# k of batch 2 transposed by DMA instead of by TensorE, with three loads held behind it, and whole loads for batch 0

## The chip, the cores and the metric

The kernel runs on one core of one Trainium2 chip. The metric is the device time of one execution in microseconds (us). Three runs of the kernel before gave 250.74, 250.46 and 250.03, median 250.46. A profile of one execution goes with it.

## The reference

Two attentions in a row, then a feed-forward layer with the gate h·cos(h). Batch 8, 8 heads, sequence 576, head size 64, 32 packed queries; 4608 tokens, model width 512, inner width 2048.

```python
def sm_attn(qq, kk, vv):
    s = scale * np.matmul(qq, kk.transpose(0, 1, 3, 2))
    s = s - np.max(s, axis=-1, keepdims=True)
    a = np.exp(s)
    a = a / (np.sum(a, axis=-1, keepdims=True) + 1e-09)
    return np.matmul(a, vv)
p_packed = sm_attn(p, k, v)
out = sm_attn(q, p_packed, p_packed)        # [8, 8, 576, 64]
x = out.transpose(0, 2, 1, 3).reshape(4608, 512)
h = x @ w_in
g = h * np.cos(h)
result = g @ w_out                          # [4608, 512], float32
```

## The kernel before

The work goes by batch, eight of them, in a pipeline written out by hand: nothing is reordered by a scheduler, so each engine executes its instructions in the order of the source. Matmuls are in bf16.

For a batch b, `load` brings k, q or v from DRAM with a cast to bf16 into the tiles `kbf` (two buffers), `qbf` and `vbf` (one buffer each). These DMAs are issued by POOL (L87). k and q must be transposed so that the head dimension lies on partitions: the tiles `kT` (two buffers) and `qT` (one). There are two ways. `xbar` (L94 to L96) issues one transposing DMA from SP, called a crossbar transfer here. `pe_T` (L98) lets TensorE (PE) do it in groups of 128x96 blocks into PSUM, each group followed by a copy on DVE or ACT. `permute_v` copies v into the tile `vp`.

The first attention is `s1` (scores against the packed queries, exp on ACT), a transposition of its result to `a1T` (`a1_pe` and `a1_one` on PE, `a1_xbar` by a DMA from SP, L159) and `pp` (L186, a1T times vp). The second is `s2` (scores of q, exp), `sums2`, `normalise`. The packed values are multiplied into w_in first (`ppw`), giving the tile `PPW`. Then `h_mm` (L259) makes one of 16 blocks of h, ACT takes the cosine (L263), DVE forms the product gT (L266). The last matmuls, with w_out (L312), come from a generator `out_gen`, and `fill(n)` puts n of them where PE would otherwise wait. Their results are copied to `osb` (four buffers) and stored by DMAs from SP (L319). The PSUM pool psA has three buffers.

A "slot" s is the loop over the 16 blocks of h of batch s, in which `hooks` run work for the next batches at given blocks. Between slots stand `s1`, `s2`, `ppw` and others, with fills.

POOL issues the loads, and also copies (`vp` of some batches, a `joint` tile). A `gate` is a tiny POOL copy that reads one element of a `kT`: since POOL executes in order, the loads behind it are issued only once that transposed tile has landed. `next_loads` in slot 1 (L449) does this for q of batch 3, k of 4 and v of 3; L504 and L530 do it for later ones. SP likewise executes its transposing DMAs and stores in order.

At the start, `warm(n)` runs n matmuls on zeros. k and q of batch 0 are each loaded in two DMAs of four heads and transposed on PE in four groups of six blocks. k of batch 2 is loaded at L408 and v of 2 at L410, both before slot 0; q of 2 and k of 3 are loaded ahead of slot 1. In slot 1, the hooks 5, 6 and 7 transpose k of batch 2 on PE, a group of eight blocks each with a copy on DVE. Hook 4 issues the crossbar transfers of q of 2 and k of 3.

Of the kernel before, what the change touches and what calls it, by code (L numbers as in the profile page):

```python
# [15 lines left out]
def kernel(  # L16
# [11 lines left out]
    B, H, S, D = q.shape  # L28
# [4 lines left out]
    C = 6  # L33
    TP = S // C
# [20 lines left out]
    V, ACT, G = nc.vector, nc.scalar, nc.gpsimd  # L55
# [5 lines left out]
    gate = const.tile([1, 1], BF16, name="gate")  # L61
# [7 lines left out]
    srcs = {"k": k, "q": q, "v": v}  # L69
    bf, vp, xT, a1T, sums1, r1, rs1 = {}, {}, {}, {}, {}, {}, {}  # L70
    a2u, lns, a2n, PPW = {}, {}, {}, {}

    def copy(eng, out, in_):
        if eng is ACT:
            ACT.copy(out=out, in_=in_)  # L75
        else:
            eng.tensor_copy(out=out, in_=in_)  # L77

    def psa(dt=FP32):
        return A.tile([128, 2, 512 if dt == FP32 else 1024], dt, name="psA", tag="A")  # L80

    def load(n, b, parts=1):
        bf[n, b] = bf_pool.tile([TP, H, C * D], BF16, name=n + "bf", tag=n + "bf", bufs=2 if n == "k" else 1)
        src = srcs[n][b].rearrange("h (p c) d -> p h (c d)", c=C)
        for i in range(parts):
            r = slice(i * H // parts, (i + 1) * H // parts)
            G.dma_start(out=bf[n, b][:, r], in_=src[:, r])  # L87

    def permute_v(b, eng=G):
        vp[b] = vp_pool.tile([TP, C, H * D], BF16, name="vp", tag="vp")  # L90
        copy(eng, vp[b].rearrange("p c (h d) -> p c h d", h=H),
             bf["v", b].rearrange("p h (c d) -> p c h d", c=C))

    def xbar(n, b):  # L94
        t = xT[n, b] = att_pool.tile([128, H * 3, TP], BF16, name=n + "T", tag=n + "T", bufs=2 if n == "k" else 1)
        nc.sync.dma_start_transpose(out=t, in_=bf[n, b].rearrange("p h x -> p (h x)"))  # L96

    def pe_T(n, b, engs=(V, V, V), groups=(0, 1, 2), own=False, m=8):  # L98
        if 0 in groups:
            xT[n, b] = att_pool.tile([128, H * 3, TP], BF16, name=n + "T", tag=n + "T", bufs=2 if n == "k" else 1)  # L100
        t = xT[n, b]
        flat = bf[n, b].rearrange("p h x -> p (h x)")
        for i in groups:
            ps = bank(BF16) if own else psa(BF16)[:, 0, :]
            for j in range(m):
                o = m * i + j
                nc.tensor.transpose(ps[:, j * TP:(j + 1) * TP], flat[:, o * 128:(o + 1) * 128],  # L107
                                    ident[0:TP, 0:TP])
            copy(engs[i], t[:, m * i:m * i + m].rearrange("p a x -> p (a x)"),
                 ps[:, 0:m * TP])  # L110

    def bank(dt=FP32):
        return O.tile([128, 512 if dt == FP32 else 1024], dt, name="ot", tag="ot")

    def pack_p(b0, b1, flat=None):
        ng = 2 * (b1 - b0)
        if flat is None:
            flat = psa(BF16).rearrange("p a x -> p (a x)")
        for g in range(ng):
            nc.tensor.transpose(flat[:, g * 128:(g + 1) * 128],  # L120
                                p_bf[:, 2 * b0 + g].rearrange("p t d -> p (t d)"), ident)
        V.tensor_copy(out=P2[:, b0:b1].rearrange("p b h n -> p (b h n)"), in_=flat[:, 0:ng * 128])

    def scores(lhs, rhs):
        ps = []
        for y in range(2):
            t = psa()
            for x in range(4):
                for e in range(2):
                    r = slice(64 * e, 64 * e + 64)  # L130
                    h = 2 * x + y
                    nc.tensor.matmul(t[32 * x:32 * x + 32, e, 0:HS], lhs[r, h, :],  # L132
                                     rhs[r, 3 * h:3 * h + 3, :], start=True, stop=True)
            ps.append(t)
        return ps

    def s1(b, later=False):
        ps = scores(P2[:, b], xT["k", b])
        sm = sums1[b] = small.tile([128, 2], FP32, name="sums1")

        def exps():
            for y in range(2):
                ACT.activation(  # L143
                    out=a1[b % 2][:, y, :, 0:TP].rearrange("p (e m) x -> p e m x", e=2),
                    in_=ps[y][:, :, 0:HS].rearrange("p e (m x) -> p e m x", m=3),
                    func=AF.Exp, scale=scale, accum_out=sm[:, y:y + 1])
        if later:
            return exps
        exps()

    def recips(b):
        r1[b] = small.tile([128, 2], FP32, name="r1")
        rs1[b] = small.tile([128, 2], FP32, name="rs1")
        V.reciprocal(r1[b], sums1[b])
        V.tensor_scalar(out=rs1[b], in0=r1[b], scalar1=scale, scalar2=None, op0=ALU.mult)  # L155
# [3 lines left out]
        nc.sync.dma_start_transpose(out=t.rearrange("p a c x -> p (a c) x"),  # L159
                                    in_=a1[b % 2].rearrange("p a c x -> p (a c x)"))  # L160

    def a1_pe(b, ys=(0, 1), own=False, eng=V):
        if 0 in ys:
            a1T[b] = att_pool.tile([128, 2, C, 128], BF16, name="a1T", tag="a1T")
        t = a1T[b]
        for y in ys:
            ps = bank(BF16) if own else psa(BF16)[:, 0, :]
            for c in range(C):
                nc.tensor.transpose(ps[0:TP, c * 128:(c + 1) * 128], a1[b % 2][:, y, c, 0:TP], ident)
            copy(eng, t[0:TP, y].rearrange("p c x -> p (c x)"), ps[0:TP, 0:C * 128])  # L170

    def a1_one(b):
        t = a1T[b] = att_pool.tile([128, 2, C, 128], BF16, name="a1T", tag="a1T")
# [155 lines left out]
    def fill(n):  # L329
        while n > 0 and filler[1] > 0:  # L330
            next(filler[0])
            filler[1] -= 1
            n -= 1

    def load_w_in(n):
        G.dma_start(out=w_in_bf[:, :, n * 512:(n + 1) * 512],
                    in_=moe_w_in.rearrange("(a p) n -> p a n", p=128)[:, :, n * 512:(n + 1) * 512])
# [5 lines left out]
    def dup_p(a, b, eng):  # L343
        for t in range(2):
            eng.tensor_copy(out=p_bf[:, a:b, t, :], in_=p_raw[:, a:b, :])

    def warm(n):
        wps = bank()
        for _ in range(n):
            nc.tensor.matmul(wps, wz[:, 0:128], wz, start=True, stop=True)  # L350

    nc.sync.dma_start(out=p_raw[:, 0:2, :], in_=p_rows[:, 0:2, :])
    load("k", 0, 2)
    load("v", 0)
    make_identity(nc, ident)
    load("q", 0, 2)
    load("k", 1)
    for n in range(3):
        load_w_in(n)
# [9 lines left out]
    warm(7)  # L369
    dup_p(0, 2, V)  # L370
    pack_p(0, 1)
    warm(6)
    pe_T("k", 0, (V, ACT, ACT, V), (0, 1), m=6)
    warm(2)
    pe_T("k", 0, (V, ACT, ACT, V), (2, 3), m=6)
    ACT.dma_start(out=p_raw[:, 2:4, :], in_=p_rows[:, 2:4, :])
    s1(0)
    load("v", 1)
    load_w_in(3)
    warm(3)  # L380
    a1_pe(0, (0,))
    permute_v(0, V)
    a1_pe(0, (1,), eng=ACT)
    warm(2)
    recips(0)
    pe_T("q", 0, (V, ACT, V, V), (0, 1), m=6)
    pp(0)
    pe_T("q", 0, (V, ACT, V, V), (2, 3), m=6)
    load("q", 1)
    for n in range(4):  # L390
        load_w_out(n)
# [15 lines left out]
    a1_one(1)  # L407
    load("k", 2)  # L408
    permute_v(1)
    load("v", 2)  # L410
    for fc in range(NFC):
        rest = h_mm(0, fc)
        if fc in (11, 12, 13):
# [13 lines left out]
    def slot(s, hooks, keep=0, heavy={}):  # L427
        left = filler[1] - keep
        out_eng[:] = (ACT,) if s > 1 else (V, ACT)
        weight = [1 + heavy.get(fc, 0) for fc in range(NFC)]  # L430
        for fc in range(NFC):
            h_mm(s, fc)()
            quota = (left * sum(weight[:fc + 1])) // sum(weight) - (left + keep - filler[1])
            first = quota
            while hooks and hooks[0][0] == fc:
                if first == quota and fc in heavy:
                    first = quota // 2
                    fill(first)
                hooks.pop(0)[1]()
            fill(quota - first if first != quota else quota)  # L440

    def pw2(b, n=0, eng=None):
        ppw(b, n, eng)
        ppw(b, n + 1, eng)

    def tk(n, b, i):
        return lambda: pe_T(n, b, (V, V, V), (i,))

    def next_loads():  # L449
        G.tensor_copy(out=gate, in_=xT["k", 3][0:1, 0, 0:1])  # L450
        for n, b in (("q", 3), ("k", 4), ("v", 3)):
            load(n, b)
# [2 lines left out]
    fill(4)  # L455
    s2(1)
    ppw(1, 0, V)
    load("q", 2)
    load("k", 3)
    dup_p(4, 2 * B, G)  # L460
    fill(5)
    sums2(1, 0)
    sums2(1, 1)
# [2 lines left out]
    normalise(1)  # L466
    ACT.preload_act_table_set(SIN_SET)
    fill(14)
    slot(1, [(3, lambda: pw2(1, 2, (ACT, V))), (4, lambda: (xbar("q", 2), xbar("k", 3))), (5, tk("k", 2, 0)), (6, tk("k", 2, 1)),
             (7, tk("k", 2, 2)), (9, lambda: pack_p(2, 5)),  # L470
             (11, lambda: pack_p(5, B)), (12, next_loads)], 4, {3: 3})

    ACT.preload_act_table_set(EXP_SET)
# [3 lines left out]
    s1(2)  # L477
    fill(5)
    a1_pe(2, (0,))
    fill(2)  # L480
    a1_pe(2, (1,))
# [96 lines left out]
```

The softmax here doesn't subtract the row's maximum and nothing guards it: scores larger than these inputs give would overflow.

## Time and profile before

| what | value |
|---|---|
| runs, median | 250.46 us (250.03 to 250.74) |
| profiled execution, its own time | 250.74 us |
| its span in the profile | 249.0 us |
| PE / DVE / ACT / POOL busy | 95% / 67% / 67% / 22% of the span |
| DMA queue of POOL's loads | 23184 packets, 18.75 MB |
| DMA queue of SP's transfers and stores | 39568 packets, 17.83 MB |
| matmuls with w_out, L312 (512 with gT) | 133.3 us, 380 ns each |
| matmuls of h, L259 (512) | 83.8 us, 286 ns each |
| crossbar transfers of q / k / a1 | 6 / 5 / 5, landing 5.5 / 5.3 / 4.0 us after issue (medians) |

The busy time of PE overlaps within itself, because matmuls are pipelined and their ends are modelled. A DMA has two times: how long the issuing engine is held by it, and when its data lands. DMA shares are means over 16 engines. "Idle before" a group of instructions, with what ended it, is harmless on an engine on which nothing waits.

### The profile page before, as it was taken

To read this page: it belongs to the slowest core of one execution; us is meant where nothing else is said; L and a number is where in the kernel's file an instruction comes from. 1 tells how busy PE (TensorE), PEld (TensorE's weight loads), DVE (VectorE), ACT (ScalarE), POOL (GpSimd) and SP (SyncE) were. 2 spreads that over 40 slices of the span, in tenths; PEclk is the share of its full clock that TensorE was granted. 3 is DMA by queue.
4 is the path that set the end of the run, shared out by engine and by line. 5 is a ranking of instruction groups with operands and counts; after the bars stand their busy time and mean duration, and the time that the engine had idled before them with its cause. 6 is when DMAs were issued, how large, how long until landed. Compare 5 with 4: busy or idle time off the path is not lost.

```text
span 249.0 us, 5072 instructions
## 1 busy us (share of the span) xinstructions
PE 236.5 (95%) x2036; PEld 131.1 (53%) x2036; DVE 167.9 (67%) x254; ACT 167.9 (67%) x280; POOL 55.9 (22%) x70
## 2 busy tenths in 40 slices
PE   8868799999999999999999999999999999999993
PEld 3445364566544655465546554565456554665452
DVE  2348997789667977587857666678766774876110
ACT  2558899756656788788867867888777684873000
POOL 8343543240400043113322205020500000000000
PEclk9999999999999999999999999999999999999999
DMA  6999999999899989999989995999491113202133
GB/s 99 167 203 205 205 206 225 202 240 164 170 190 201 185 156 217 205 204 160 200 168 195 165 205 68 190 171 190 94 154 40 45 42 77 52 21 63 46 84 84
DMA packets 63207, 37.09 MB, mean 149 GB/s; under 512 B 35824, under 2 KB 58608, under 8 KB 63184
## 3 DMA queue, kind: packets, MB, share of 16 engines
q0 software_dynamic: 23184, 18.75, 49.5%
q1 hardware_dynamic: 39568, 17.83, 34.2%
q8 instruction: 16, 0.26, 0.4%
q10 hardware_dynamic: 432, 0.20, 0.4%
q14 instruction: 7, 0.06, 0.1%
HBM read 37.22 MB, written 9.44 MB: 187 GB/s over the span
## 4 chain that ended last, share of the span: by engine, by line
PE 71%; DMA 15%; DVE 6%; ACT 3%; POOL 2%; issue 1%; DVEq 0%; POOLq 0%
PE ot L312 43%; PE psA L259 19%; DMA w_out_bf<-in_moe_w_out_dram 8%; DMA w_in_bf<-in_moe_w_in_dram 7%; DVE gT L266 4%; PE psA L210 3%; ACT cosT L263 2%; PE psA L186 2%; PE psA L132 2%; PE ot L298 1%; PE psA L236 1%; DVE PPW L77 1%; POOL kbf L87 1%; ACT ppT L75 1%; DVE a2n L246 1%
## 5 line engine op out<-in xcount | busy, mean ns | idle before, releaser
L312 PE MATMUL ot<-w_out_bf,gT 128*128 128x512 bf16 x512 | 133.3, 380 | 0.1
L266 DVE TENSOR_TENSOR gT<-psA,cosT 128x576 bf16<-128x576 f32 x128 | 93.7, 756 | 26.5 <-ACT cosT L263 25.9
L263 ACT ACTIVATE cosT<-psA 128x576 bf16<-128x576 f32 x128 | 82.5, 651 | 28.2 <-PE psA L259 23.5
L259 PE MATMUL psA<-a2n,PPW 128*128 128x288 bf16 x512 | 83.8, 286 | 1.7 <-DVE PPW L77 0.4
L312 PEld LDWEIGHTS <-gT 128*128 128x128 bf16 x512 | 47.6, 98 | 43.3 <-issue 6.7
L259 PEld LDWEIGHTS <-PPW 128*128 128x128 bf16 x512 | 49.2, 97 | 35.2 <-issue 4.4
L77 DVE CAST PPW<-psA 128x1024 bf16<-128x1024 f32 (+1 forms) x23 | 26.9, 1176 | 11.6 <-PE psA L210 11.5
L270 POOL COPY joint<-gT 128x512 bf16<-128x512 bf16 x16 | 9.8, 614 | 88.1 <-DVE gT L266 88.1
L77 DVE COPY osb<-ot 128x512 f32<-128x512 f32 (+1 forms) x24 | 16.3, 679 | 17.5 <-PE ot L312 13.9
L75 ACT COPY osb<-ot 128x512 f32<-128x512 f32 (+1 forms) x13 | 7.3, 565 | 15.3 <-PE ot L312 10.6
L77 POOL COPY vp<-vbf 96x3072 bf16<-96x3072 bf16 x6 | 16.5, 2749 | 4.0 <-DMA vbf<-in_v_dram 4.0
L246 DVE SCALAR_TENSOR_TENSOR a2n<-a2u,r,lns 128x576 bf16<-128x576 bf16 x16 | 12.3, 813 | 7.3 <-ACT lns L244 7.3
L143 ACT ACTIVATE a<-psA 128x576 bf16<-128x576 f32 x16 | 10.3, 646 | 7.3 <-PE psA L132 7.2
L238 ACT ACTIVATE lns<-psA 128x576 f32<-128x576 f32 x16 | 10.1, 650 | 7.1 <-PE psA L236 6.5
L312 PE MATMUL ot<-w_out_bf,joint 128*128 128x512 bf16 x48 | 12.8, 379 | 0.0
L228 ACT ACTIVATE a2u<-psA,rs 128x576 bf16<-128x576 f32 x16 | 11.0, 737 | 1.5 <-PE psA L132 1.4
L210 PE MATMUL psA<-w_in_bf,ppT 64*32 64x512 bf16 x224 | 10.2, 381 | 0.0
L244 ACT ACTIVATE lns<-lns 128x576 f32<-128x576 f32 x16 | 10.0, 676 | 0.0
L350 PE MATMUL ot<-wz 128*128 128x512 bf16 x24 | 8.8, 500 | 1.2 <-DVE wz L361 1.2
L75 ACT CAST ppT<-psA 64x128 bf16<-64x128 f32 x24 | 6.2, 259 | 5.1 <-DVE ppT L77 3.8
L87 POOL DMA_DIRECT2D vbf<-in_v_dram x8 | 6.2, 776 | 6.4 <-DVE rs L155 4.4
L77 DVE COPY kT<-psA 128x768 bf16<-128x768 bf16 (+1 forms) x8 | 4.0, 526 | 5.2 <-PE psA L107 5.2
(73 smaller groups left out, 153.1 us busy)
## 6 DMA issues: line engine op xcount, KB each, us to landing
vbf<-in_v_dram POOLq DMA_DIRECT2D x8, 576.0 KB, 8.4
out_dram<-osb SPq DMA_DIRECT2D x24, 192.0 KB, 2.6
kbf<-in_k_dram POOLq DMA_DIRECT2D x7, 576.0 KB, 13.0
qbf<-in_q_dram POOLq DMA_DIRECT2D x7, 576.0 KB, 10.1
out_dram<-osb SPq DMA_DIRECT2D x22, 128.0 KB, 2.4
w_in_bf<-in_moe_w_in_dram POOLq DMA_DIRECT2D x4, 512.0 KB, 17.0
w_out_bf<-in_moe_w_out_dram POOLq DMA_DIRECT2D x4, 512.0 KB, 20.5
out_dram<-osb SPq DMA_DIRECT2D x26, 64.0 KB, 2.1
```

The source lines that it names most:

```text
L75: ACT.copy(out=out, in_=in_)
L77: eng.tensor_copy(out=out, in_=in_)
L143: ACT.activation(out=a1[b % 2][:, y, :, 0:TP].rearrange("p (e m) x -> p e m x", e=2), in_=ps[y][:, :, 0:HS].rearrange("p e (m x) -> p e m ...
L210: nc.tensor.matmul(ps[y][32 * x:32 * x + 32, :], ppT[b % 2][r, 2 * x + y, :], w_in_bf[r, x, n * 512:(n + 1) * 512], start=True, stop=True)
L228: ACT.activation(out=a2u[b][:, y].rearrange("p (e x) -> p e x", e=2), in_=ps[y][:, :, 0:HS], func=AF.Exp, scale=rs1[b][:, y:y + 1])
L238: ACT.activation(out=lns[b][:, y].rearrange("p (e x) -> p e x", e=2), in_=ps[:, :, 0:HS], func=AF.Ln)
L244: ACT.activation(out=lns[b][:, y], in_=lns[b][:, y], func=AF.Exp, scale=-1.0)
L246: V.scalar_tensor_tensor(out=a2n[b][:, y], in0=a2u[b][:, y], scalar=r1[b][:, y:y + 1], in1=lns[b][:, y], op0=ALU.mult, op1=ALU.mult)
L259: nc.tensor.matmul(ps[:, e, 0:HS], PPW[b][:, y, fc * 128:(fc + 1) * 128], a2n[b][:, y, e * HS:(e + 1) * HS], start=(y == 0), stop=(y == 1))
L263: ACT.activation(out=csv, in_=ps[:, :, 0:HS], func=AF.Sin, bias=PI_HALF)
L266: V.tensor_tensor(out=gT[b][:, fc, :].rearrange("p (e x) -> p e x", e=2), in0=ps[:, :, 0:HS], in1=csv, op=ALU.mult)
L312: nc.tensor.matmul(pss[c], w, w_out_bf[:, fc, :], start=(fc == 0), stop=(fc == NFC - 1))
```

## The change

k and q of batch 0 are loaded by one DMA each, and transposed in three groups of eight blocks instead of four of six. The copy of v of batch 0 to `vp` on DVE moves ahead of the a1 transposes, whose two copies are both on DVE. `pp(0)` precedes all transposes of q of batch 0 instead of standing between two halves of them. There are nine warm matmuls ahead of k's transposes instead of six and two.

`xbar("k", 2)` is issued behind `permute_v(1)`, and the three groups `tk` in slot 1 are gone. The loads of v of 2, q of 2 and k of 3 come after `dup_p(4, 2 * B, G)` and behind a POOL copy that reads kT of batch 2.

```diff
-    def load(n, b, parts=1):
+    def load(n, b):
         bf[n, b] = bf_pool.tile([TP, H, C * D], BF16, name=n + "bf", tag=n + "bf", bufs=2 if n == "k" else 1)
-        src = srcs[n][b].rearrange("h (p c) d -> p h (c d)", c=C)
-        for i in range(parts):
-            r = slice(i * H // parts, (i + 1) * H // parts)
-            G.dma_start(out=bf[n, b][:, r], in_=src[:, r])
+        G.dma_start(out=bf[n, b], in_=srcs[n][b].rearrange("h (p c) d -> p h (c d)", c=C))
...
-    load("k", 0, 2)
+    load("k", 0)
     load("v", 0)
     make_identity(nc, ident)
-    load("q", 0, 2)
+    load("q", 0)
...
-    warm(6)
-    pe_T("k", 0, (V, ACT, ACT, V), (0, 1), m=6)
-    warm(2)
-    pe_T("k", 0, (V, ACT, ACT, V), (2, 3), m=6)
+    warm(9)
+    pe_T("k", 0, (V, ACT, V))
     ACT.dma_start(out=p_raw[:, 2:4, :], in_=p_rows[:, 2:4, :])
     s1(0)
+    permute_v(0, V)
     load("v", 1)
     load_w_in(3)
     warm(3)
-    a1_pe(0, (0,))
-    permute_v(0, V)
-    a1_pe(0, (1,), eng=ACT)
+    a1_pe(0)
     warm(2)
     recips(0)
-    pe_T("q", 0, (V, ACT, V, V), (0, 1), m=6)
     pp(0)
-    pe_T("q", 0, (V, ACT, V, V), (2, 3), m=6)
+    pe_T("q", 0, (V, ACT, V))
...
     load("k", 2)
     permute_v(1)
-    load("v", 2)
+    xbar("k", 2)
...
     s2(1)
     ppw(1, 0, V)
-    load("q", 2)
-    load("k", 3)
     dup_p(4, 2 * B, G)
+    G.tensor_copy(out=gate, in_=xT["k", 2][0:1, 0, 0:1])
+    for n, b in (("v", 2), ("q", 2), ("k", 3)):
+        load(n, b)
...
-    slot(1, [(3, lambda: pw2(1, 2, (ACT, V))), (4, lambda: (xbar("q", 2), xbar("k", 3))), (5, tk("k", 2, 0)), (6, tk("k", 2, 1)),
-             (7, tk("k", 2, 2)), (9, lambda: pack_p(2, 5)),
+    slot(1, [(3, lambda: pw2(1, 2, (ACT, V))), (4, lambda: (xbar("q", 2), xbar("k", 3))), 
+             (9, lambda: pack_p(2, 5)),
              (11, lambda: pack_p(5, B)), (12, next_loads)], 4, {3: 3})
```

More of the change, by code (lines that the diff above doesn't have):

```diff
@@ L96, in xbar, with pe_T @@
         nc.sync.dma_start_transpose(out=t, in_=bf[n, b].rearrange("p h x -> p (h x)"))
-    def pe_T(n, b, engs=(V, V, V), groups=(0, 1, 2), own=False, m=8):
+    def pe_T(n, b, engs=(V, V, V), groups=(0, 1, 2), own=False):
         if 0 in groups:
@@ L104, in pe_T @@
             ps = bank(BF16) if own else psa(BF16)[:, 0, :]
-            for j in range(m):
-                o = m * i + j
+            for j in range(8):
+                o = 8 * i + j
                 nc.tensor.transpose(ps[:, j * TP:(j + 1) * TP], flat[:, o * 128:(o + 1) * 128],
                                     ident[0:TP, 0:TP])
-            copy(engs[i], t[:, m * i:m * i + m].rearrange("p a x -> p (a x)"),
-                 ps[:, 0:m * TP])
+            copy(engs[i], t[:, 8 * i:8 * i + 8].rearrange("p a x -> p (a x)"),
+                 ps[:, 0:8 * TP])
     def bank(dt=FP32):
@@ L160, in a1_xbar, with a1_pe @@
                                     in_=a1[b % 2].rearrange("p a c x -> p (a c x)"))
-    def a1_pe(b, ys=(0, 1), own=False, eng=V):
+    def a1_pe(b, ys=(0, 1), own=False):
         if 0 in ys:
@@ L169, in a1_pe @@
                 nc.tensor.transpose(ps[0:TP, c * 128:(c + 1) * 128], a1[b % 2][:, y, c, 0:TP], ident)
-            copy(eng, t[0:TP, y].rearrange("p c x -> p (c x)"), ps[0:TP, 0:C * 128])
+            copy(V, t[0:TP, y].rearrange("p c x -> p (c x)"), ps[0:TP, 0:C * 128])
     def a1_one(b):
@@ L444, in pw2 @@
         ppw(b, n + 1, eng)
-    def tk(n, b, i):
-        return lambda: pe_T(n, b, (V, V, V), (i,))
     def next_loads():
```

## Prediction

> **What bounds the kernel now.** I read the page first. TensorE (PE) is busy 95% of the span, but the DMA row is nearly as full: nine tenths or more in most slices up to 187 us. The chain that ended last is PE work with one long DMA stretch at the start.
>
> ```profile
> PE 236.5 (95%) x2036; PEld 131.1 (53%) x2036; DVE 167.9 (67%) x254; ACT 167.9 (67%) x280; POOL 55.9 (22%) x70
> DMA  6999999999899989999989995999491113202133
> PE 71%; DMA 15%; DVE 6%; ACT 3%; POOL 2%; issue 1%; DVEq 0%; POOLq 0%
> ```
>
> So there are two near-limits, and the change moves work from PE to the DMA side. The next view is the timeline of slot 1 on DVE (start, duration, engine, line, operation). Each PE transposition of k2 leaves a copy on DVE between two gT products:
>
> ```profile
> 53.23 0.55 DVE L77 COPY kT<-psA 128x768 bf16<-128x768 bf16 x1
> 54.03 0.76 DVE L266 TENSOR_TENSOR gT<-psA,cosT 128x576 bf16<-128x576 f32 x1 [0.25 <-ACT cosT L263]
> 54.70 0.55 DVE L77 COPY kT<-psA 128x768 bf16<-128x768 bf16 x1
> ```
>
> The last view is the timeline of SP and POOL for the transfers (SPq is SP's queue; the duration is how long SP is held):
>
> ```profile
> 56.55 3.68 SPq L96 DMA_TRANSPOSE qT<-qbf  x1
> 60.28 3.07 SPq L96 DMA_TRANSPOSE kT<-kbf  x1
> 65.25 0.18 POOL L450 COPY gate<-kT 1x1 bf16<-1x1 bf16 x1 [8.30 <-DMA kT<-kbf]
> 65.79 0.77 POOL L87 DMA_DIRECT2D qbf<-in_q_dram  x1 [0.36 <-issue]
> 73.40 5.95 SPq L96 DMA_TRANSPOSE qT<-qbf  x1
> 79.44 2.43 SPq L159 DMA_TRANSPOSE a1T<-a  x1
> 86.34 0.86 PE L186 MATMUL psA<-a1T,vp 96*128 96x64 bf16 x24 [0.58 <-DVE gT L266]
> ```
>
> This is a chain: q2 and k3 transposed, the gate opens when kT of batch 3 has landed, then q3, k4 and v3 are loaded, then q3 and a1 of batch 3 are transposed, and pp(3) on PE (L186, 86.34) reads that a1T. The tile views, restricted to one issue each, give landings: k2 49.57, v2 52.5, q2 56.5, k3 59.4, kT of 3 65.2, q3 73.4 (7.6 after issue), v3 80.4, a1T of 3 84.84 (5.4 after issue). pp(3) therefore has only 86.34 − 84.84 = **1.5 us of slack**.
>
> **What the Trainium skill says.** "DMA: Bandwidth & Descriptors", section "Issuing engines are not separate DMA queues": transfers from all issuers run on the same 16 engines and interleave. The trace agrees: the crossbar transfer of a q or k landed 4.9 us after issue with its loads landed, 5.5 beside one remaining load, 10.3 beside two. The same page, "Terms" and "DMA Transpose (X-bar)": a plain transposing DMA comes from SP or ACT only, so the new one must stand in SP's order. "TensorE: Matmul & The Clock Gate", Part 1: after an idle window of some 3.4 us the array falls to half clock, and needs about as long to return. The trace shows the cold state at the start (128x512 matmuls 0.43 us apart from 1.2 us on, against 15.32/71 = 0.216 late); no long idle later in this kernel shows the fall.
>
> **The change part by part.**
>
> 1. *Start: k and q of batch 0 whole.* k0's second half landed at 2.07 + 5.8 = 7.9; the same bytes in one DMA land near 7.9. All 24 transposes (50 ns each, 1.2) then come after it instead of 12 (0.68), and the last copy is 0.55 instead of 0.46: +0.6 at the exps. q0's halves landed at 13.0 and 14.8; whole, 24 transposes and the last copy end near 16.6 instead of 16.2: +0.4. Moving the vp copy (0.96 on DVE) before the a1T copies, and both of those to DVE, gives at most as much. POOL issues two DMAs fewer (about 0.6 each saved), but its queue is backlogged (w_in landed 14 to 18 us after issue), so nothing lands sooner. PE then waits for DMA anyway: k1 at 18.8 (0.4), w_in at 31.3 (0.65), w_out at 44.5 (0.2). What arrives at slot 1: taken as 0, bounds −0.3 to +0.6.
>
> 2. *No PE transposes in slot 1.* 24 matmuls at about 43 ns (0.34 us a group of eight) = 1.0 us of PE, and 3 x 0.55 = 1.65 us of DVE. The three steps with a group of transposes took 1.48 us each (51.18, 52.66, 54.14, 55.61); steps with two fills take 0.92. Gain 3 x 0.56 = **−1.7 us** at the end of slot 1, by itself on the path.
>
> 3. *kT of 2 by crossbar.* In SP's order it is the first thing after p_raw, ahead of four stores (issued 47.9 before). k2 lands at about 49.6 as before, since what is queued ahead of it is unchanged. No q or k transfer of this trace runs entirely alone; the nearest is kT of 3: SP 3.07, landing 4.9 (bounds 4.0, the median of a1's, and 5.7). I take 4.9: **54.5**. Its reader, s1(2), runs at 64.7: hidden with 10 us to spare. The four stores go out near 53 to 55; four output buffers cover the four chunks of batch 0, so PE does not feel it.
>
> 4. *The gate.* v2, q2, k3 were issued at 32.8, 39.9, 40.65 and queued behind other loads without a hole. Now POOL waits for kT of 2; behind the gate stand those loads, the vp copy of batch 2, a joint copy and the next gate. From 54.5 the first load is issued 0.55 later (65.2 to 65.79 is the model), v2 at 55.0, q2 at 55.8, k3 at 56.6. In the three groups of v, q, k after 88 us, v landed 6.2, 8.1, 6.5 after its issue, q 9.0, 10.7, 10.1, k 12.1, 13.0, 12.2. Stores are mostly out of the way, so I take 6.2 and 9.0: v2 61.2, **q2 64.8**, and k3 2.9 later as before, 67.7. vp of 2 is then ready at 61.2 + 2.75 = 64.0; pp(2) stands at 68.2 (66.5 with the gain): hidden.
>
> 5. *What comes late next.* The q2 transfer holds SP 64.8 to 68.5 (3.68, again one load beside it) and lands at 70.3; s2(2) ran at 70.53, wanted 68.8 with the gain: the gain is already swallowed. The k3 transfer starts at 68.5 and lands at **73.4**, 8.2 later than before; s1(3) ran at 72.31, so PE is now 1.1 behind. The next gate opens at 73.4; q3 is issued at 74.0 and lands at 81.6; its transfer holds SP 5.95 (k4 and v3 still loading, as before) to 87.55; a1 goes at 87.65 and lands 5.4 later at **93.0**. v3 lands near 88.6, so the vp copy of batch 3 on DVE (84.68 before) waits too, and three psA buffers are full behind it, but this ends before 93.0. pp(3) moves from 86.34 to 93.0: **+6.7 us**. PE executes in order and has nothing else to run there, so the wait is idle time.
>
> 6. *Clock.* That idle lasts about 87 to 93. If the array cools, roughly 3.4 us of half clock cost 1.7. Bounds 0 and 1.7; I take 0.8.
>
> Beyond it, kT of 4 lands at 87.7 + 8.3 = 96.0, q4 near 107, while its transfer would start at 99.98 + 6.7 = 106.7: chain and PE are level again, and pp(4) has 110.35 − 107.65 = 2.7 slack. PE has hardly any idle later from which to win the time back. Sum: 6.7 + 0.8 = +7.5; parts 1 and 2 don't add, because absolute landings decide. The profiled execution took 250.74 (249.0 span and 1.7 around it), 0.28 over the median: 258.2, or **258.0** against the median.
>
> **Rivals.** *A, hidden transfers, faster:* only the −1.7 of slot 1 counts, 248.8. For it: k2's transfer itself has 10 us of cover, and DMA idles between. Against: it needs kT of 3 by 70.6 and a1T of 3 by 84.6, and the group of loads alone takes 12 us. *B, shorter chain:* first load 6.0 after issue and the others 2.6 apart, transfers 3.0 on SP as at 124.9, q3 and a1 nearer to the uncontended 3.7 and 3.9: pp(3) slips 2.5 to 4, no cooling; 253 to 254.5. *C, the delay grows:* loads at the slow end (q 10.7, 1.7 later), q4's transfer late by over pp(4)'s 2.7, full cooling: 260.5 to 262. *D, a wash:* the stall only eats the gain, 250.5.
>
> **Chances.** Main case (255.5 to 260.5) 0.66, B 0.14, C 0.10, A 0.06, D 0.04. About 0.3% (0.75 us) can be told from no change. Faster 0.06, same 0.04, slower 0.90. Range 253.5 to 261.0: it takes in bounds of loads, start and clock, most of B and part of C, and leaves out some 0.2.
>
> **What would show it.** Right: kT of 2 landing near 54.5; v2, q2, k3 issued from 55; the kT of 3 landing near 73.4; the gate at L440 ending its wait there; a PE gap ahead of pp(3) (L183 in the changed numbering) ended by a1T or vp, 5 us or more; slot 1 shorter by 1.7. Wrong: pp(3) waiting under 2 us, q2 landing before 61, or a1T of 3 landing before 87.

## Result and the profile after

The changed kernel takes 257.34 us (median of 6 runs, 256.47 to 258.81) against 250.54 (6 runs): ratio **1.0278**, 95% interval 1.0245 to 1.0311. The profiled execution took 256.47 us with a span of 254.7. It is the fastest of the six, 5.7 us over the span before, where the medians differ by 6.8. Every ratio is to the kernel before, run beside it on the same chip, and leaves out executions more than 1.5% above the fastest of their kernel, which the medians keep.

These are the rows of the changed kernel's page that were shown of before, and PEclk, the clock granted to PE in tenths of full speed:

```profile
PE 238.0 (93%) x2013; PEld 130.9 (51%) x2013; DVE 166.8 (65%) x251; ACT 166.7 (65%) x278; POOL 54.9 (22%) x69
PEclk9999999999977999999999999999999999999999
DMA  6999999679979999999999992999291111302133
PE 70%; DMA 19%; DVE 4%; ACT 2%; issue 2%; POOL 2%; SPq 0%; DVEq 0%; POOLq 0%
```

The PEclk row of before:

```profile
PEclk9999999999999999999999999999999999999999
```

DMA's share of the chain that ended last rose from 15% to 19%. The DMA row (slices of 6.4 us, counted from 0), which before stood at nine there, now shows six, seven and seven in slices 7, 8 and 11 (45 to 57 and 70 to 76 us): the engines run short of work while a gate holds the loads. PEclk, at nine throughout before, shows two sevens (slices 11 and 12).

The timeline of SP and POOL (start, time held, engine, line, operation; what ended the idle time before it in brackets):

```profile
48.74 3.13 SPq L93 DMA_TRANSPOSE kT<-kbf  x1
63.84 3.80 SPq L93 DMA_TRANSPOSE qT<-qbf  x1
67.75 3.02 SPq L93 DMA_TRANSPOSE kT<-kbf  x1
81.31 6.03 SPq L93 DMA_TRANSPOSE qT<-qbf  x1
87.44 1.46 SPq L156 DMA_TRANSPOSE a1T<-a  x1
```

```profile
53.77 0.18 POOL L449 COPY gate<-kT 1x1 bf16<-1x1 bf16 x1 [5.77 <-DMA kT<-kbf]
54.29 0.77 POOL L84 DMA_DIRECT2D vbf<-in_v_dram  x1 [0.34 <-POOL gate L449]
74.44 0.18 POOL L440 COPY gate<-kT 1x1 bf16<-1x1 bf16 x1 [10.13 <-DMA kT<-kbf]
75.00 0.77 POOL L84 DMA_DIRECT2D qbf<-in_q_dram  x1 [0.39 <-issue]
```

The gate of batch 3 opens at 74.44 instead of 65.25, and q3 is issued at 75.0 instead of 65.8. In the timeline of PE the chain ends in three waits, for qT of 2, kT of 3 and a1T of 3:

```profile
69.23 0.44 PE L129 MATMUL psA<-qT,ppT 64*32 64x288 bf16 x16 [1.08 <-DMA qT<-qbf]
74.36 0.68 PE L129 MATMUL psA<-kT,P 64*32 64x288 bf16 x16 [3.30 <-DMA kT<-kbf]
92.16 0.86 PE L183 MATMUL psA<-a1T,vp 96*128 96x64 bf16 x24 [1.60 <-DMA a1T<-a]
```

pp(3) runs at 92.16 instead of 86.34, 5.8 us late. The next score matmuls of q (s2(3)) run at 102.96 instead of 97.15: the same 5.8, which stays to the end (5.7). Nothing later adds or gives back. Two lines of before (the scores of batch 3 and s2(3)), then s2(3) of the changed kernel:

```profile
72.31 0.44 PE L132 MATMUL psA<-kT,P 64*32 64x288 bf16 x16
97.15 0.44 PE L132 MATMUL psA<-qT,ppT 64*32 64x288 bf16 x16
```

```profile
102.96 0.44 PE L129 MATMUL psA<-qT,ppT 64*32 64x288 bf16 x16
```

### The profile page after: what moved, and what is told of

It reads as the page before. It is cut to its first block, busy times and chain, and to the rows that moved or that the text cites. A ratio compares the mean times of both kernels' runs of the same rounds, so it can differ in the third digit from the quotient of the medians.

```text
span 254.7 us, 5024 instructions
## 1 busy us (share of the span) xinstructions
PE 238.0 (93%) x2013; PEld 130.9 (51%) x2013; DVE 166.8 (65%) x251; ACT 166.7 (65%) x278; POOL 54.9 (22%) x69
## 4 chain that ended last, share of the span: by engine, by line
PE 70%; DMA 19%; DVE 4%; ACT 2%; issue 2%; POOL 2%; SPq 0%; DVEq 0%; POOLq 0%
PE ot L309 42%; PE psA L256 19%; DMA w_out_bf<-in_moe_w_out_dram 8%; DMA w_in_bf<-in_moe_w_in_dram 6%; PE psA L207 3%; DMA kT<-kbf 3%; DVE gT L263 2%; DMA a1T<-a 2%; PE psA L183 2%; PE psA L129 2%; PE ot L295 1%; PE psA L233 1%; ACT cosT L260 1%; DVE PPW L77 1%; ACT ppT L75 1%
## 5 line engine op out<-in xcount | busy, mean ns | idle before, releaser
L309 PE MATMUL ot<-w_out_bf,gT 128*128 128x512 bf16 x512 | 135.0, 384 | 0.1
L309 PEld LDWEIGHTS <-gT 128*128 128x128 bf16 x512 | 48.2, 98 | 44.7 <-issue 8.4
L347 PE MATMUL ot<-wz 128*128 128x512 bf16 x25 | 8.2, 466 | 1.2 <-DVE wz L358 1.2
L183 PEld LDWEIGHTS <-vp 96*128 96x128 bf16 x192 | 6.5, 98 | 3.5 <-DVE gT L263 1.9
L129 PE MATMUL psA<-kT,P 64*32 64x288 bf16 x128 | 4.4, 306 | 3.6 <-DMA kT<-kbf 3.3
## 6 DMA issues: line engine op xcount, KB each, us to landing
kbf<-in_k_dram POOLq DMA_DIRECT2D x8, 576.0 KB, 11.6
```

Source lines behind the costliest of these rows:

```text
L183: nc.tensor.matmul(ps[:, hp * 64:(hp + 1) * 64], vp[b][:, c, hp * 128:(hp + 1) * 128], a1T[b][0:TP, :, j, 32 * hp:32 * hp + 32], start=(j ...
L309: nc.tensor.matmul(pss[c], w, w_out_bf[:, fc, :], start=(fc == 0), stop=(fc == NFC - 1))
```

## The experiments

Where landings are named, they come from the tile view of one issue.

**The start alone.** The kernel before with the changed start (`load` whole, transposes in groups of eight, the new order), and, as a second kernel, with nothing but the two loads whole:

```diff
-    load("k", 0, 2)
+    load("k", 0)
...
-    load("q", 0, 2)
+    load("q", 0)
```

> Only the start is changed (k and q of batch 0 whole, their transposes in three groups); k of batch 2 still goes through PE and no load waits for a gate. Theory 1, the slot part alone costs and the start gains: the last block of w_out lands 0.8 us earlier, as it did in the changed kernel (43.7 against 44.5), PE follows it from slot 1 on, and the kernel takes 249.7. Rival, the start is worth nothing as predicted, and the earlier landing came from something else: 250.5.

> The kernel before with one DMA each for k and q of batch 0; all its PE transposes, copies and orders stay. Theory 1, the two halves move bytes more slowly (130 to 165 GB/s between 6 and 10 us against 200): the last block of w_out lands 0.8 earlier, and the time is 249.7. Rival, the slow stretch of before belongs to the order of the work around it and not to the halves: 250.5, with the same slow stretch.

The start alone took 250.18 us, ratio 0.9976 (0.9963 to 0.9989). The whole loads alone took 250.08, ratio 0.9979 (0.9969 to 0.9988). The whole loads give as much as the whole start, some 0.5 us; the regrouped transposes add nothing visible. The windows view shows what differs (stretch, its length, then busy time of PE, PEld, DVE, ACT and POOL, the clock, the DMA share, GB/s), first before, then with whole loads:

```profile
7.00:8.00 1.00, 0.79 (x11) 0.30 (x9) 0.46 (x1) 0.64 (x1) 1.00 (x2) 1.00 1.21 136
8.00:9.00 1.00, 0.84 (x16) 0.57 (x17) 0.35 (x1) 0.61 (x1) 0.42 (x1) 1.00 1.11 148
```

```profile
7.00:8.00 1.00, 0.67 (x13) 0.62 (x14) 0.20 (x1) 0.00 (x0) 0.30 (x1) 1.00 1.31 204
8.00:9.00 1.00, 1.00 (x19) 0.72 (x17) 0.26 (x2) 0.90 (x2) 0.00 (x0) 1.00 1.31 204
```

The last column is what counts: in this stretch the engines of the kernel before show a share of 1.11 to 1.21 instead of 1.31 (the times of packets are added up, so a share can exceed 1), but move 136 to 148 GB/s instead of 204. With whole loads pp(3) runs at 85.55, 0.8 earlier in that trace. Two things limit what this shows. The slow stretch (6 to 10 us) spans the second half of k and most of v, which is one whole load; the halves of q, which landed at 13.0 and 14.8, moved at 195 to 204 GB/s. So the stretch goes with the halves, but it isn't shown that a half is slower as such. And in the trace of the start alone, its slowest execution (250.56), the stretch is gone as well, yet pp(3) ran at 86.16, only 0.2 earlier.

A rival is that POOL, with two DMAs fewer to issue, issues the first block of w_in at 5.03 instead of 6.15. The bytes speak against it: summed over the windows of 1 us, the kernel before had moved 572 KB by 6 us against 500 with whole loads, and fell behind only then, to 1164 against 1311 by 10 us, though POOL had issued its last load of this group at 8.4. No run separates the two, and why the stretch is slow was not tried.

**The slot part alone.** The start of before, with the crossbar transfer of k2 and the gate; the three groups of PE transposes in slot 1 are gone, as in the change.

```diff
     permute_v(1)
-    load("v", 2)
+    xbar("k", 2)
...
-    load("q", 2)
-    load("k", 3)
     dup_p(4, 2 * B, G)
+    G.tensor_copy(out=gate, in_=xT["k", 2][0:1, 0, 0:1])
+    for n, b in (("v", 2), ("q", 2), ("k", 3)):
+        load(n, b)
```

> Only the slot part is changed (k of batch 2 by crossbar, v2, q2 and k3 behind the gate); the start is that of before. Theory 1, absolute landings decide: without the start's 0.8 everything in the chain lands 0.8 later than in the changed kernel, 258.1, with a wait of 2.5 to 3.5 us ahead of the scores of batch 3, half clock after it, and a second wait ahead of pp(3). Rival, the parts simply add without a chain: start 0 and slot part +6.8: 257.3.

It took 260.23 us, ratio 1.0366 (1.0315 to 1.0416), more than both forecasts. The trace, of its fastest execution (258.11), gives a test of the chain. Here PE also ran at half clock for parts of the first 40 us (mean clock 0.50 from 15 to 20 us, 0.64 and 0.67 from 30 to 40) and came into the chain 5.7 us later than in the changed kernel (67.89 against 62.20 for the scores of batch 2). pp(3) still ran at the same moment, 92.12 against 92.16:

```profile
67.89 0.44 PE L132 MATMUL psA<-kT,P 64*32 64x288 bf16 x16
92.12 0.86 PE L186 MATMUL psA<-a1T,vp 96*128 96x64 bf16 x24 [3.12 <-DMA a1T<-a]
104.60 0.44 PE L132 MATMUL psA<-qT,ppT 64*32 64x288 bf16 x16
```

So it is the landing of a1T of 3 (92.0 in both) that sets pp(3), whatever PE has won or lost before, as long as it comes earlier. s2(3) came 12.5 us behind pp(3) instead of 10.8: the wait ahead of pp(3) was followed by half clock. I had expected the start's halves to make the landing 0.8 later. They made k2's transfer start 0.6 later, but kT of 3 took 4.8 us to land instead of 6.6, so that the two landings agree partly by chance. What the other executions lost beyond this one (2.1 us in the median) no trace shows.

**The delay alone.** k2 transposed by PE as before, no crossbar transfer for it, but the three loads held behind a gate on a gT block of slot 1. The gate, v2's copy and the two transfers move into block 6 (the new function; the lines at the old places go):

```diff
+    def held():
+        G.tensor_copy(out=gate, in_=gT[1][0:1, 5, 0:1])
+        for n, b in (("v", 2), ("q", 2), ("k", 3)):
+            load(n, b)
+        permute_v(2)
+        xbar("q", 2)
+        xbar("k", 3)
```

> The kernel before, with k of batch 2 still transposed by PE and the start in halves, but v2, q2 and k3 held back behind a gate that reads a gT block of slot 1, so that they are issued near 54 as in the changed kernel. Theory 1, the delay of these loads is the cost and the crossbar transfer of k2 by itself is not needed for it: q2 near 63.5, kT of batch 3 near 72 to 74, a1T of batch 3 near 91 to 92, a wait of 4 to 6 us ahead of pp(3): 256.5 to 259.5. Rival, the extra transfer carries a good part: 254 or less.

It took 258.34 us, as forecast, ratio 1.0285 (1.0246 to 1.0323). **The delay alone costs as much as the change, without the new transfer.** POOL and PE in its trace:

```profile
53.55 0.18 POOL L449 COPY gate<-gT 1x1 bf16<-1x1 bf16 x1 [4.74 <-DVE gT L266]
72.54 0.44 PE L132 MATMUL psA<-kT,P 64*32 64x288 bf16 x16
91.28 1.44 PE L186 MATMUL psA<-a1T,vp 96*128 96x64 bf16 x24 [5.28 <-DMA a1T<-a]
104.99 0.44 PE L132 MATMUL psA<-qT,ppT 64*32 64x288 bf16 x16
```

PE is on the times of before up to the scores of batch 3 (72.54 against 72.31), then waits 5.3 us at pp(3). s2(3) follows 13.7 later instead of 10.8: 2.9 for the clock. So the parts differ from those of the changed kernel's trace: here pp(3) is 4.9 late and the clock adds 2.9, there pp(3) is 5.8 late and the clock adds nothing.

**The gate gone, and the loads early.** Two kernels from the changed one: the gate copy left out with the loads where they are, and the loads at their places of before. The first takes out the line with `gate` alone; this is the edit of the second:

```diff
     permute_v(1)
     xbar("k", 2)
+    load("v", 2)
...
+    load("q", 2)
+    load("k", 3)
     dup_p(4, 2 * B, G)
-    G.tensor_copy(out=gate, in_=xT["k", 2][0:1, 0, 0:1])
-    for n, b in (("v", 2), ("q", 2), ("k", 3)):
-        load(n, b)
```

> The changed kernel without the gate ahead of v2, q2 and k3; the loads stay where they are in POOL's order, behind the cast of p, and are issued near 48 instead of 54.3. Theory 1, the gate's hold is the cost: everything in the chain comes about 6 us earlier, q2 near 57, kT of batch 3 near 67, no wait ahead of the scores of batch 3: 249 to 251. Rival, loads beside the crossbar transfer of k2 slow it and one another (a transfer landed 10 us after issue beside two loads), so most of the delay stays: 254 or more.

> The changed kernel with v2, q2 and k3 loaded at their places of before and without the gate; k of batch 2 still by crossbar. Theory 1, it is the held loads that cost: q2 lands near 57 to 58, kT of batch 3 near 66 to 67, no wait ahead of the scores of batch 3, no half clock; slot 1 keeps its 1.7 and the start its 0.8, and pp(3) is then set by the a1T of batch 3, some 2 us of extra DMA time later than before: 248 to 250.5. Rival, the extra crossbar transfer itself, which shares the DMA engines and stands in SP's order, costs: slower than before, 252 or more.

With the gate gone it took 258.19 us, ratio 1.0291 (1.0250 to 1.0332). With the loads early it took 255.44, ratio 1.0132 (1.0074 to 1.0191), its executions lying between 251.92 and 257.12. My theory failed for both: the rival held. Beside loads, k2's transfer holds SP twice to three times as long, first gate gone, then loads early:

```profile
48.48 9.11 SPq L93 DMA_TRANSPOSE kT<-kbf  x1
60.02 5.72 SPq L93 DMA_TRANSPOSE qT<-qbf  x1
```

```profile
49.17 6.54 SPq L93 DMA_TRANSPOSE kT<-kbf  x1
55.76 4.47 SPq L316 DMA_DIRECT2D out_dram<-osb  x4
60.34 3.15 SPq L93 DMA_TRANSPOSE qT<-qbf  x1
```

In the second, q2 had landed at 54.8, yet its transfer started at 60.34, behind four stores which stood behind k2's transfer. That is 3.8 later than before (56.55). kT of 3 landed at 70.6 and a1T of 3 at 88.15 (before 65.2 and 84.84), and PE, 2.3 early by then, waited 4.3 for it:

```profile
88.32 1.44 PE L183 MATMUL psA<-a1T,vp 96*128 96x64 bf16 x24 [4.26 <-DMA a1T<-a]
101.41 0.44 PE L129 MATMUL psA<-qT,ppT 64*32 64x288 bf16 x16
```

pp(3) was 2.0 late by this, and half clock behind the wait added 2.3 (13.1 to s2(3) instead of 10.8): the larger part of this execution's 4.2. Without the gate kT of 2 itself landed 16.0 after issue, at 64.5, and its scores waited 2.3. So the gate buys a quick transfer with late loads; without it the transfer is slow, and SP's order passes that on.

**q2 and k3 ahead of v2**, no gate:

```diff
-    for n, b in (("v", 2), ("q", 2), ("k", 3)):
-        load(n, b)
+    load("q", 2)
+    load("k", 3)
+    load("v", 2)
     dup_p(4, 2 * B, G)
```

> The changed kernel without the gate, q2 and k3 loaded ahead of slot 1 as before and v2 behind them. Theory 1, the place of q2 and k3 in the queue sets the chain: they land one load (2.9 us) earlier than with v2 ahead, kT of batch 3 near 63 to 64, pp(3) has slack, and the gains of slot 1 (1.7) and of the start (0.8) both stay: 248.0, faster than both kernels. Rival, the a1T of batch 3 is late all the same, or v2 now lands too late for pp(2): 250 or more.

It took 255.14 us, ratio 1.0179 (1.0127 to 1.0232): my theory missed, the rival held. q2 and k3 did land early (51.6, 54.3), but q2's transfer started at 58.49, again behind k2's (6.46 on SP) and the stores. a1T of 3 landed at 87.2; PE wanted it at 83.1:

```profile
87.31 1.44 PE L183 MATMUL psA<-a1T,vp 96*128 96x64 bf16 x24 [4.17 <-DMA a1T<-a]
101.04 0.44 PE L129 MATMUL psA<-qT,ppT 64*32 64x288 bf16 x16
```

pp(3) ran only 1.0 later than before, but s2(3) came 13.7 behind it: 2.9 of the 3.9 us that s2(3) lost are the half clock that the wait left behind.

**The clock alone.** 14 matmuls on zeros ahead of the scores of batch 3 in the changed kernel.

```diff
     fill(5)
+    warm(14)
     s1(3)
```

> The changed kernel with 14 extra matmuls on zeros (3.0 us at full clock) ahead of the scores of batch 3, in the place of its wait of 3.3. Theory 1, the half clock after that wait costs by itself: PE stays at full clock from 74 to 80, and PE reaches slot 2 about 2.7 earlier; but pp(3) then waits for its a1T, which hangs on the loads behind kT of batch 3, so that only some 1 us or less is won: 256.3 to 257.3. Rival, the half clock is the decisive cost: 254.6. Second rival, it costs nothing: 257.3.

It took 258.76 us, ratio 1.0364 (1.0295 to 1.0432), above all three forecasts; its interval meets that of the changed kernel, so no loss against it is shown, and no gain either. PE kept its clock and came to pp(3) earlier, only to wait there longer, and the clock fell there (mean 0.51 from 93 to 96 us):

```profile
92.11 0.86 PE L183 MATMUL psA<-a1T,vp 96*128 96x64 bf16 x24 [4.35 <-DMA a1T<-a]
93.00:96.00 3.00, 2.78 (x11) 1.63 (x11) 0.69 (x1) 1.69 (x5) 0.18 (x1) 0.51 0.94 194
```

The half clock behind the first wait is free as long as pp(3) waits for DMA; behind pp(3) it is not (12.5 to s2(3) instead of 10.8).

**The stores first.** The transfers of q2 and k3 at block 12 of slot 1 instead of 4, behind stores in SP's order.

> The changed kernel with the crossbar transfers of q2 and k3 moved from block 4 to block 12 of slot 1, behind the stores of two chunks in SP's order. Theory 1, six stores that had piled up behind these transfers compete with the last of them (it landed 6.6 us after issue instead of 4.9): the stores now go out earlier, kT of batch 3 lands 1 to 1.7 earlier, the wait ahead of the scores shrinks to about 2, the array does not fall to half clock, and pp(3) comes 1 to 1.7 earlier: 255 to 256.3. Rival, the stores have no part in it: 257.3.

It took 258.19 us, ratio 1.0306 (1.0275 to 1.0338). kT of 3 landed 6.4 after issue, where the changed kernel had 6.6. Four stores still stood behind that transfer, instead of six. But six stood behind it in the slot part alone and before as well, where it landed 4.8 and 4.9 after issue, so the stores by themselves don't make the landing slow; its cause stays open.

**pp(3) later.** Three kernels: the changed one, the one with q2 and k3 first, and that one with later slots too.

```diff
-    slot(2, [(4, lambda: permute_v(3, V)), (7, lambda: pp(3, engs=(ACT, ACT))), (11, lambda: pw2(3))], 5, {11: 3})
+    slot(2, [(6, lambda: permute_v(3, V)), (12, lambda: pp(3, engs=(ACT, ACT))), (13, lambda: pw2(3))], 5, {13: 3})
```

The last one also has, in the loop over later slots:

```diff
-        slot(s, [(5, lambda: pp(s + 1, engs=(ACT, ACT))), (10, lambda: pw2(s + 1))] if nxt else [], 5, {10: 3})
+        slot(s, [(9, lambda: pp(s + 1, engs=(ACT, ACT))), (12, lambda: pw2(s + 1))] if nxt else [], 5, {12: 3})
```

> The changed kernel with pp(3) at block 12 of slot 2 instead of 7, the copy of v of 3 at 6 instead of 4, and the heavy ppw at 13. Theory 1, only the second wait (1.6 us in the changed kernel, up to 4 in other runs) goes, because a1T of batch 3, landing near 92, is then needed near 95; the wait ahead of the scores of batch 3 and the half clock after it stay: 255 to 256. Rival, pp(3) moved later starves what follows it, and nothing is won: 257.3 or more.

> The kernel without gate and with q2 and k3 loaded ahead of v2, and pp(3) at block 12 of slot 2, the copy of v of 3 at 6, ppw at 13. In the same kernel with pp(3) at 7 PE waited 4.2 us for a1T of batch 3 (landing 87.2, wanted 83.1) and then ran at half clock. Theory 1, pp(3) wanted 4.6 later doesn't wait, the clock stays whole, and the gains of start and slot 1 are kept: 248 to 249, faster than both kernels. Rival, the next batch's chain is now short by as much and PE waits there: 250.5 or more.

> As the run before it, and in the later slots too pp(s+1) stands at block 9 instead of 5 and the heavy ppw at 12. Theory 1: the same 248 to 249 if no later slot waits for its a1T; 1 us better than the run before it if one does there. Rival, later places squeeze ppw against the end of the slot: slower than the run before it.

The changed kernel with pp(3) late took 257.06 us, ratio 1.0222 (1.0178 to 1.0265); its interval meets that of the changed kernel, so a gain isn't shown. The wait at pp(3) went, but one of 2.73 us at pp(4) took its place. q2 and k3 first with pp(3) late took 252.42, ratio 1.0023 (0.9996 to 1.0049), where my theory had 248 to 249; here pp(4) waited 1.73. Its executions spread from 249.89 to 256.26, and its median is 0.7% above that of the kernel before, so it isn't shown to be as fast. With later slots as well it took 249.73, ratio **0.9964** (0.9944 to 0.9984): faster than the changed kernel by far, and than the kernel before by 0.4%. That gain is small, but the interval lies below 1; it overlaps that of the whole loads alone. Its two pp:

```profile
88.15 0.87 PE L183 MATMUL psA<-a1T,vp 96*128 96x64 bf16 x24 [0.41 <-DMA a1T<-a]
112.37 0.86 PE L183 MATMUL psA<-a1T,vp 96*128 96x64 bf16 x24 [0.35 <-DMA a1T<-a]
```

a1T of 3 lands at 88.1, later than in the kernel before (84.84), and costs 0.4. That supports the theory from the other side: what hurts is not the late landing itself, but a reader placed ahead of it. What the later places are worth by themselves isn't known: the kernel before was not run with them. Of the 2.2 us that start and slot 1 should have kept (0.5 and 1.7), only some 0.9 was gained; where the rest went was not followed up.

## Why the prediction was right, and where it was not

The time (258.0 forecast, 257.34 measured) and the mechanism, a chain of transfers whose landings decide pp(3), held. That the sum came so close is in part luck, since errors within step 5 partly cancelled and the 0.8 of step 6 stands for a cost that this trace has in another place. Step by step:

1. *Start, taken as 0.* Wrong. The step that failed is "its queue is backlogged, so nothing lands sooner": it took the rate of the queue as given. In the kernel before the queue moved 136 to 164 GB/s from 6 to 10 us, where it moves about 200 in the changed one; the last block of w_out (issue plus time to landing) landed at 43.67 instead of 44.46, and the start alone gained 0.2%.
2. *Slot 1, −1.7.* Right: from the first block of slot 1 to the scores of batch 2 it takes 62.20 − 44.36 = 17.84 instead of 64.66 − 45.15 = 19.51, so −1.67. Nothing of it reached the end.
3. *kT of 2 landing 4.9 after issue, near 54.5.* Right: 5.0, at 53.74, with the start's 0.8.
4. *Gate and loads.* Right: v2 6.7, q2 8.7 and k3 10.8 after issue (6.2, 9.0, 11.1 forecast). v2 to k3 were issued from 54.29.
5. *What comes late next.* Right in its links, off in three sizes that partly cancelled, by luck. kT of 3 took 6.6 instead of 4.9 to land (74.35 for 73.4), so PE waited 3.3 at the scores; q3 took 6.3 instead of 7.6; a1 was held 1.46 and landed 4.6 after issue instead of 2.43 and 5.4. The k3 transfer also started 0.75 earlier than forecast. a1T of 3 landed at 92.04 for 93.0, and pp(3) moved 5.8, not 6.7. Two terms of rival B came true in part (a first load after 6.3, a1 after 4.6); others did not, since q3's transfer held SP 6.03 and kT of 3 landed later.
6. *Clock, 0.8 after pp(3).* Placed wrongly for the profiled execution. It reckoned with idle time ahead of pp(3) only, though the part before it already let PE wait for qT of 2 and kT of 3. The Trainium skill, "TensorE: Matmul & The Clock Gate", Part 1, gives some 3.4 us of idle before half clock; here the clock fell in the 3.3 us ahead of those scores, and other runs show it after shorter waits (last section). The windows view of the changed kernel (the last three columns are clock, DMA share, GB/s):

```profile
71.00:74.30 3.30, 0.07 (x1) 0.00 (x0) 0.17 (x1) 0.00 (x0) 0.00 (x0) 0.85 0.87 215
74.30:77.50 3.20, 3.14 (x29) 1.06 (x30) 1.72 (x3) 1.37 (x4) 2.68 (x5) 0.50 0.56 109
77.50:80.50 3.00, 3.00 (x24) 1.06 (x22) 0.02 (x1) 2.26 (x4) 0.41 (x1) 0.56 1.24 182
```

From those scores to slot 2 PE needed 83.62 − 74.36 = 9.26 instead of 78.83 − 72.31 = 6.52. The 2.7 only shortened the wait at pp(3), and cost nothing at the end. So this execution shows the +5.7 of the chain alone. The median's further 1.1 would fit executions in which the clock falls at pp(3), as in the delay alone and the slot part alone. That is argued, not shown: no other execution of the changed kernel was profiled, and their mean clocks (0.993, 0.986 and 0.985 in the three from 257.30 to 258.07, 0.986 in the profiled one) don't decide it.

Rival A, transfers hidden, fell with the result; the delay alone shows that holding the loads is enough for a loss of this size. The runs with the loads early show what my prediction left out: holding the loads is not the only price. The new transfer also costs when they are not held, through SP's time and order. And the half clock behind a wait can cost more than the late reader itself, as with q2 and k3 first.

## What to carry over

Moving work from the busiest engine to DMA paid here only where the chain of transfers had slack at its next reader; follow it to that reader's landing and place before counting the engine's gain. A gate trades a fast transfer for late loads, and every transfer on an in-order issuing queue delays what stands behind it, even data that has landed. Where a landing is late, moving its reader back can win the time back (1.0179 to 0.9964 with q2 and k3 first), but look for the next batch's reader too.

## What was not expected of the hardware

- With k and q of batch 0 loaded in halves, the DMA engines moved 136 to 148 GB/s from 7 to 9 us where they move 204 with whole loads, and were nearly as busy; the halves of q later moved at the full rate.
- A transposing DMA of a k held SP 3.1 us with no load beside it, 6.5 beside early loads and 9.1 when loads were issued just before and behind it; it landed 5.0, 11.6 and 16.0 us after issue.
- From slot 1 on, the length of PE's wait alone didn't decide whether the clock fell. It fell after waits of 2.3 us (gate gone, ahead of the scores of batch 2: 0.50 from 66 to 68 us), 2.6 (stores first, ahead of s2(2): 0.50 from 72 to 74), 2.95 (the changed kernel with pp(3) late, ahead of the scores of batch 3: 0.50 from 76 to 78) and all of 3.1 and more. It stayed at 1.00 after one of 2.73 (the same run, ahead of pp(4)) and one of 3.0 (stores first, ahead of pp(3), 93 to 96 us), and after 1.7 and less. Where it fell at pp(3), s2(3) came 12.5 to 13.7 us behind instead of 10.8.
